# Score products of an attention kernel on 32x32 tiles of TensorE instead of 32x128 tiles

## The chip, the cores and the metric

The kernel runs on one core of one Trainium2 chip. The metric is the device time of one execution, in microseconds (us). Three executions of the kernel before took 753.29, 753.73 and 753.77 us; the median is 753.73 us.

## What is computed

x is 2048 rows of 640 (bf16). Two branches work on it, and a gate mixes them for each row:

```python
g = sigmoid((x * gate_w).sum(-1))
qkv = (x @ wqkv).reshape(S, 3, H, Dh)       # S=2048, H=32 heads, Dh=20
p = softmax(q @ k.T * Dh**-0.5)             # for each head
a = (p @ v).reshape(S, 640) @ wo
h = x @ w1 + b1                             # 640 -> 1536
b = (h * tanh(softplus(h))) @ w2            # 1536 -> 640
out = g * a + (1 - g) * b
```

## The kernel before, in words

**Layout.** x, k and q lie transposed in SBUF: `xT` with 640 rows in five blocks of 128, `kT` and `qT` with four heads stacked in the 128 partitions. Each head has a strip of 32 partitions, of which 20 hold data and the rest are zero. Four such heads are a quad; there are eight quads. Queries go in four chunks of 512 (QC), keys in 16 tiles of 128. A pair of quad and query chunk is a group (GROUPS, line 51), 32 groups in all, and a group has 32 units: one unit is one key tile for one pair of heads (`uinfo`, line 194), so there are 1024 units.

**A unit.** TensorE multiplies the strip of 32 rows of `kT` of a head (128 keys, the weights) with the strip of `qT` of that head (512 queries, the moving data) into one PSUM bank of 128 keys x 512 queries. A unit has two such products, for two heads, into the two banks of a slot. PSUM has eight banks: three slots of two, one bank that accumulates p @ v (ACCB), and one for other work (MISC). The scores of a slot are then turned into exp by ScalarE (line 946, 728 units) or by VectorE with an integer approximation of exp (line 966, 296 units), which makes three bf16 terms of a unit: the first by VectorE from PSUM, the two others from the first by GpSimd or VectorE (line 1065). Those results wait in the SBUF rings `EA` and `EC`.

**p @ v.** For each unit, `emit_pv` (line 662) multiplies 32 columns of `VA` (20 of v, a column of ones for the denominator, padding) with the exp tile of 128 keys x 512 queries, and accumulates in ACCB. The four heads of a quad go to the four strips of 32 partitions of that bank.

**Shapes on TensorE.** TensorE's array is addressed with a tile position (row, column). `mm` (line 299) is the only place that issues the matmuls; all of them carry line 300 in the profile. Three shapes occur:

- Score products use 32 rows x 128 columns at position (32r, 0), r being the head's place in the quad. Four of them, with four values of r, cover the array. The planner issues one unit (two products) or two units (four products) at a time.
- Everything else that multiplies, p @ v and the projections and the dense branch (through `mm4`, line 302), uses 128 rows x 32 columns at (0, 32q). Four of these cover the array.
- Transposes of x at the start (line 310) and in the last microseconds use the whole array, 128 x 128.

**The order of the work.** It is not found at run time. `make_plan` (line 220) simulates the five engines with a clock of its own (`Clock`, line 113) and writes down one list of calls, which is then issued in that order under a manual schedule; the waits follow from the data. `pe_run` (line 589) charges a burst of four products 217 ns, and 111 ns more when the kind of work changes between score products ("R"), products of 32 columns ("C") and transposes ("T"). `poll_pe` (line 826) asks in this order: score products if two slots are free or ScalarE is about to run dry, then p @ v if the exp rings are nearly full, then other work that is due, then p @ v. These charges are constants in the plan's code; the order of work that comes out doesn't depend on what `emit_score` (line 599) issues.

Of the kernel before, what the change touches and what calls it, by code (L numbers as in the profile page):

```python
# [10 lines left out]
P = 128  # L11
# [9 lines left out]
QC, NQC = 512, 4  # L21
# [172 lines left out]
def uinfo(n):  # L194
    g, k = divmod(n, 32)
    p, c = GROUPS[g]
    return g, p, c, k // 2, k % 2
# [22 lines left out]
def make_plan(K, par):  # L220
# [78 lines left out]
    def mm(o, l, r, first, last, pos):  # L299
        K.nc.tensor.matmul(o, lhsT=l, rhs=r, start=first, stop=last, tile_position=pos, skip_group_check=True)  # L300
# [298 lines left out]
    def emit_score(n, slot):  # L599
        g, p, c, kt, pair = uinfo(n)  # L600

        def fn():
            for t in range(2):
                r = 2 * pair + t
                mm(
                    K.ps[:, 2 * slot + t, :],
                    K.kT[32 * r : 32 * r + 32, p % 3, kt * P : (kt + 1) * P],
                    K.qT[32 * r : 32 * r + 32, p % 3, c * QC : (c + 1) * QC],
                    True,
                    True,  # L610
                    (32 * r, 0),
                )

        emit(fn)

# [733 lines left out]
```

## Time and profile before

| what | value | from |
|---|---|---|
| time of the profiled execution | 752.86 us | its result |
| its span, first to last instruction | 751.0 us | the page's head |
| around the span | 1.86 us | difference |
| median of three runs | 753.73 us | the times |
| mean granted clock of TensorE | 0.994 | the view of cores |
| busy: DVE, ACT, POOL | 587.7, 712.4, 532.0 us | part 1 |
| DMA | 41.86 MB, 56 GB/s on the mean | the page |
| instructions fetched by DMA (queue q8) | 82 packets, 1.34 MB | part 3 |

The page gives for each group of instructions its line, engine, shape and count, then the busy time with the mean duration of one in ns, then the time its engine stood idle before it. Matmuls overlap: one of 512 columns is shown as some 380 ns long, while the next can start after 216 ns or, on another tile, after a few ns. What tells the pace of TensorE is therefore the distance from start to start, not the duration, and these starts are in the trace's timeline.

### The profile page before, as it was taken

Reading aid. Unit: us, or ns where it says so; the run is one execution under the profiler, and the core shown is the slowest. Engines: PE = TensorE matmul, PEld = TensorE weight load, DVE = VectorE, ACT = ScalarE, POOL = GpSimd, SP = SyncE. Lnnn points to the kernel's source line nnn. Section 1 sums busy time; section 2 is a strip of 40 time slices with the busy share of each in tenths; the row PEclk is TensorE's granted clock in tenths of the full one; section 3 lists DMA queues with packets and bytes.
Section 4 is the critical chain, followed back from the end, with each engine's and each line's share of the span. In section 5 each row is a group of like instructions: output and inputs, shape, how many; then the busy total and the mean of one; then the engine's idle time right before and its main releaser. Section 6 shows DMA issues by size and latency. Waiting matters only on the chain.

```text
span 751.0 us, 25003 instructions
## 1 busy us (share of the span) xinstructions
PE 725.0 (97%) x10480; PEld 254.5 (34%) x10480; DVE 587.7 (78%) x758; ACT 712.4 (95%) x753; POOL 532.0 (71%) x496
## 2 busy tenths in 40 slices
PE   5989999999999999999999999999989999999997
PEld 3423333222233333333333333222323333333335
DVE  2486777878788787888878879888878887887794
ACT  2989999999999999999999999999999999999993
POOL 9155677766788676777767777777787688657773
PEclk8999999999999999999999999999999999999999
DMA  9242210002101001121111210000233110221132
GB/s 292 102 130 68 75 43 19 18 30 63 22 21 41 27 29 42 42 81 32 35 37 43 66 30 21 17 14 14 73 91 101 30 35 25 69 69 45 58 103 76
DMA packets 45722, 41.86 MB, mean 56 GB/s; under 512 B 20120, under 2 KB 39240, under 8 KB 45608
## 3 DMA queue, kind: packets, MB, share of 16 engines
q1 hardware_dynamic: 42984, 39.94, 17.9%
q8 instruction: 82, 1.34, 0.8%
q10 hardware_dynamic: 2624, 0.31, 0.3%
q14 instruction: 32, 0.26, 0.1%
HBM read 27.59 MB, written 12.38 MB: 53 GB/s over the span
## 4 chain that ended last, share of the span: by engine, by line
PE 77%; ACT 9%; DVE 8%; issue 3%; DMA 2%; POOL 0%; SPq 0%; ACTq 0%; DVEq 0%
PE ps L300 77%; ACT EA L946 8%; DVE EC L966 5%; DMA wv<-in_gate_w_dram 2%; DVE EC L1065 1%; DVE accs L989 1%; PE ps L310 0%; DVE VA L404 0%; DVE act L425 0%; POOL EC L1065 0%; DMA den<-accs 0%; DVE stg L357 0%; SPq L1146 0%; ACT L905 0%; DVE gt L936 0%
## 5 line engine op out<-in xcount | busy, mean ns | idle before, releaser
L946 ACT ACTIVATE EA<-ps 128x1024 bf16<-128x1024 f32 x728 | 680.0, 1045 | 24.0 <-PE ps L300 20.5
L1065 POOL TENSOR_SCALAR EC<-EC 128x1024 uint16<-128x1024 uint16 x426 | 468.7, 1101 | 202.7 <-DVE EC L966 176.8
L966 DVE TENSOR_SCALAR EC<-ps 128x1024 uint16<-128x1024 f32 x296 | 361.1, 1221 | 95.4 <-PE ps L300 72.6
L300 PE MATMUL ps<-qT,kT 32*128 32x512 bf16 x2048 | 290.4, 384 | 8.6 <-DVE EC L966 2.7
L300 PE MATMUL ps<-EC,VA 128*32 128x512 bf16 x1776 | 237.2, 384 | 1.7 <-DVE accs L989 1.1
L300 PE MATMUL ps<-EA,VA 128*32 128x512 bf16 x1456 | 207.4, 383 | 0.4 <-DVE accs L989 0.4
L300 PEld LDWEIGHTS <-kT 32*128 32x128 bf16 x2048 | 76.5, 91 | 262.5 <-issue 255.8
L300 PEld LDWEIGHTS <-VA 128*32 128x32 bf16 x3232 | 76.4, 95 | 92.3 <-issue 78.2
L1065 DVE TENSOR_SCALAR EC<-EC 128x1024 uint16<-128x1024 uint16 x166 | 93.4, 563 | 7.5 <-DVE EC L966 0.5
L300 PE MATMUL ps<-R,act 128*32 128x320 bf16 x1536 | 84.1, 302 | 0.1
L300 PE MATMUL ps<-xT,R 128*32 128x512 bf16 x960 | 79.3, 384 | 1.0 <-DVE act L425 1.0
L300 PEld LDWEIGHTS <-R 128*32 128x32 bf16 (+1 forms) x1728 | 41.7, 95 | 45.6 <-issue 34.9
L300 PEld LDWEIGHTS <-act 128*32 128x32 bf16 x1536 | 36.1, 95 | 36.4 <-issue 27.4
L300 PE MATMUL ps<-wv,xT 128*32 128x81 bf16 (+2 forms) x960 | 35.3, 263 | 5.9 <-DMA wv<-in_gate_w_dram 5.5
L425 DVE TENSOR_SCALAR act<-ps,b1f 128x512 bf16<-128x512 f32 x48 | 35.7, 744 | 3.1 <-PE ps L300 2.8
L357 DVE CAST stg<-ps 128x512 bf16<-128x512 f32 (+1 forms) x40 | 27.3, 683 | 8.8 <-PE ps L300 8.8
L300 PE MATMUL ps<-wk,R 128*32 128x320 bf16 (+1 forms) x640 | 33.6, 302 | 0.1
L300 PE MATMUL ps<-xT,wk 128*32 128x512 bf16 x360 | 32.8, 383 | 0.1
L1167 POOL TENSOR_TENSOR ons<-accs,rb 128x512 bf16<-128x512 f32 x24 | 31.1, 1294 | 2.5 <-DMA rb<-rd_d 1.1
L300 PE MATMUL ps<-xT,wq 128*32 128x512 bf16 x400 | 30.5, 382 | 1.1 <-DVE VA L404 1.1
L404 DVE CAST VA<-ps 128x80 bf16<-128x80 f32 (+2 forms) x48 | 16.3, 373 | 15.7 <-PE ps L300 15.7
L300 PEld LDWEIGHTS <-xT 128*32 128x32 bf16 x960 | 18.7, 99 | 20.0 <-issue 12.1
(69 smaller groups left out, 200.9 us busy)
## 6 DMA issues: line engine op xcount, KB each, us to landing
rb<-rd_d SPq DMA_DIRECT2D x124, 64.0 KB
qd<-stg SPq DMA_DIRECT2D x20, 128.0 KB
b_d<-bst SPq DMA_DIRECT2D x16, 160.0 KB
out_dram<-ost SPq DMA_DIRECT2D x16, 160.0 KB
kT<-kd SPq DMA_DIRECT2D x28, 80.0 KB
qT<-qd SPq DMA_DIRECT2D x28, 80.0 KB
stg<-b_d SPq DMA_DIRECT2D x13, 160.0 KB
kd<-stg SPq DMA_DIRECT2D x16, 128.0 KB
```

Of the source, the lines that this page charges most:

```text
L300: K.nc.tensor.matmul(o, lhsT=l, rhs=r, start=first, stop=last, tile_position=pos, skip_group_check=True)
L357: K.nc.vector.tensor_copy(out=K.stg[0:w, s, :], in_=bank(b)[0:w, :])
L404: K.nc.vector.tensor_copy(out=K.VA[:, t0 + i, h0 * VS : (h0 + nh) * VS].rearrange("p (h d) -> p h d", d=VS)[:, :, 0:DH], in_=src[:, i, 0 : ...
L425: K.nc.vector.tensor_scalar(out=K.act[:, f, (c % 2) * QC : (c % 2 + 1) * QC], in0=bank(b), scalar1=K.b1f[:, f : f + 1], scalar2=None, op0= ...
L946: lambda: K.nc.scalar.activation(K.EA[:, e, :], K.ps[:, 2 * slot : 2 * slot + 2, :].rearrange("p b n -> p (b n)"), ACT.Exp, scale=SCALE)
L966: lambda: K.nc.vector.tensor_scalar(out=K.EC[:, e, :], in0=K.ps[:, 2 * slot : 2 * slot + 2, :].rearrange("p b n -> p (b n)"), scalar1=CH_M ...
L989: emit(lambda: K.nc.vector.tensor_copy(out=K.accs[:, g % 2, :], in_=K.ps[:, ACCB, :]))
L1065: eng.tensor_scalar(out=K.EC[:, e, :], in0=K.EC[:, e0, :], scalar1=float(CH_ADD[k]), scalar2=1.0, op0=ALU.add, op1=ALU.mult)
L1167: gp_q.append((1350.0, lambda: K.nc.gpsimd.tensor_tensor(out=dst(), in0=K.accs[:, b, :], in1=K.rb[:, b, :], op=ALU.mult), lambda: pl.give( ...
```

## The change

Each score product of 128 keys becomes four products of 32 keys. Product q takes 32 columns of the same 32 rows of `kT`, streams the same 512 columns of `qT`, and writes partitions 32q to 32q+31 of the same PSUM bank, at tile position (32r, 32q). The loop over the strips q is inside the loop over the two heads t. So a unit issues 8 products with 8 weight loads instead of 2 with 2, and two units together 16 with 16 instead of 4 with 4. Nothing else is edited.

```diff
             for t in range(2):
                 r = 2 * pair + t
-                mm(
-                    K.ps[:, 2 * slot + t, :],
-                    K.kT[32 * r : 32 * r + 32, p % 3, kt * P : (kt + 1) * P],
-                    K.qT[32 * r : 32 * r + 32, p % 3, c * QC : (c + 1) * QC],
-                    True,
-                    True,
-                    (32 * r, 0),
-                )
+                for q in range(4):
+                    mm(
+                        K.ps[32 * q : 32 * q + 32, 2 * slot + t, :],
+                        K.kT[32 * r : 32 * r + 32, p % 3, kt * P + 32 * q : kt * P + 32 * q + 32],
+                        K.qT[32 * r : 32 * r + 32, p % 3, c * QC : (c + 1) * QC],
+                        True,
+                        True,
+                        (32 * r, 32 * q),
+                    )
```

The lists of instructions of both kernels stand in the same order on every engine. On TensorE 2048 score products with their loads become 8192, so that its list grows from 20955 to 33243 rows. The lists of the other engines don't change but for line numbers (every line behind the edit moves by one).

## The prediction

> **What bounds the kernel now.** I read the page's busy times, then the chain of work that ended last, then the groups of line 300, then TensorE's timeline.
>
> ```profile
> PE 725.0 (97%) x10480; PEld 254.5 (34%) x10480; DVE 587.7 (78%) x758; ACT 712.4 (95%) x753; POOL 532.0 (71%) x496
> PE 77%; ACT 9%; DVE 8%; issue 3%; DMA 2%; POOL 0%; SPq 0%; ACTq 0%; DVEq 0%
> L946 ACT ACTIVATE EA<-ps 128x1024 bf16<-128x1024 f32 x728 | 680.0, 1045 | 24.0 <-PE ps L300 20.5
> L300 PE MATMUL ps<-qT,kT 32*128 32x512 bf16 x2048 | 290.4, 384 | 8.6 <-DVE EC L966 2.7
> L300 PEld LDWEIGHTS <-kT 32*128 32x128 bf16 x2048 | 76.5, 91 | 262.5 <-issue 255.8
> L300 PEld LDWEIGHTS <-VA 128*32 128x32 bf16 x3232 | 76.4, 95 | 92.3 <-issue 78.2
> ```
>
> TensorE carries 77% of the chain, ScalarE (ACT) 9%, VectorE 8%. ACT is nearly as full (95%), so TensorE getting slower costs at once, while TensorE getting faster soon meets ACT. A busy share doesn't tell how tight TensorE is; start-to-start distances do. First a stretch of the dense branch mixed with attention (columns: start us, length us, group):
>
> ```profile
> 360.99 0.39 PE L300 MATMUL ps<-EC,VA 128*32 128x512 bf16 x4
> 361.20 0.31 PE L300 MATMUL ps<-R,act 128*32 128x320 bf16 x4
> 361.44 0.40 PE L300 MATMUL ps<-qT,kT 32*128 32x512 bf16 x4
> 361.77 0.59 PE L300 MATMUL ps<-R,act 128*32 128x320 bf16 x12
> 362.19 0.39 PE L300 MATMUL ps<-EA,VA 128*32 128x512 bf16 x4
> 362.40 0.39 PE L300 MATMUL ps<-EC,VA 128*32 128x512 bf16 x4
> 362.73 0.39 PE L300 MATMUL ps<-qT,kT 32*128 32x512 bf16 x2
> ```
>
> Bursts of 32-column products of 512 follow each other every 0.21 us (360.99, 361.20), which is the streaming of 512 columns, and those of 320 every 0.14. Into a score burst it takes 0.33 us (362.40 to 362.73), and out of it 0.33 (361.44 to 361.77). To the nanosecond, the medians in the trace are: 216 between bursts of 32 columns, 322 from such a burst of 512 to a score burst, 318 out of a score burst of two products and 325 out of one of four, 226 instead of 216 behind the first burst after a score burst. Products of one burst start 3.5 ns apart. So every number is a stream of 213 ns, plus 3.5 ns for each product behind the first, plus **a pause of 98 ns at each change of shape**; a change there and back costs 98 + 98 + 10 = 206 ns.
>
> Score bursts come in 717 visits: 416 of two products, 262 of four, 39 of several bursts. In all there are 496 bursts of two and 264 of four (992 + 1056 = 2048, the row's count). Of the 717 visits 662 start within 15 ns of that model, so 92% of them wait for nothing but TensorE itself.
>
> **Does the pause go?** The change keeps the columns of the shape (32 wide everywhere) and leaves the rows different (32 for scores, 128 for the rest). Before has no products of 32x32, so the pause is bounded by the nearest rows: 206 ns a visit if rows alone make it, nothing if columns alone do. The transposes (line 310) tell: they are 128x128, and differ from a score product in rows only.
>
> ```profile
> 19.49 0.39 PE L300 MATMUL ps<-qT,kT 32*128 32x512 bf16 x2
> 19.81 0.56 PE L310 MATMUL ps<-ident,act 128*128 128x128 bf16 x7
> 20.31 0.39 PE L300 MATMUL ps<-qT,kT 32*128 32x512 bf16 x2
> ```
>
> Both have all 128 columns; only rows change, and yet it takes 0.32 us out of the score burst (19.49 to 19.81), the same as to 32-column work. In the other direction two such changes take 151 and 152 ns from a transpose, which streams 53 ns: 98 again. From transposes to 32-column work, where columns alone change, it is 149. Each of the two by itself brings the whole pause. I take 98 ns unchanged on both sides: this edit saves nothing there. What speaks against it is that all these rows involve transposes, which may pause for a reason of their own.
>
> The Trainium skill, "TensorEngine Tiling (Array Packing)", section Key Properties, says that changing the tiling mode, and not just the tile, drains TensorE, and it lists 32x32 and 128x32 as different modes. By it the sum has no saving either; the transposes' 151 and 320 ns agree, and no run so far shows 32x32.
>
> **What the change adds.** A burst of two becomes eight products and a burst of four sixteen: 496 x 6 + 264 x 12 = 6144 more products with as many loads. The moving data of the sixteen tiles stream together, as four tiles of different rows do now, and four of different columns do. But the shape changes behind the last, so the last start counts: 318 to 325 ns for two more products shows 3.5 ns for each. 6144 x 3.5 = **21.5 us** on TensorE: 21 ns for a burst of two, 42 for one of four.
>
> The Trainium skill, "TensorE: Matmul & The Clock Gate", section The mechanism, gives some 4 ns between starts of tiles; by that the sum would be 24.6 us.
>
> What is hidden: where TensorE waits for ACT or VectorE anyway, the 21 or 42 ns vanish. 92% of visits have no such wait, which gives 19.8 us; by the chain's 77% it is 16.6. I take 18 between them. ACT and VectorE get their scores 21 to 42 ns later, which costs nothing of its own while TensorE is the bound.
>
> **Costs taken as nothing.** (1) Issuing. Sixteen pairs of load and product must be issued within a visit:
>
> ```profile
> 27.78 0.52 PE L300 MATMUL ps<-wv,xT 128*32 128x81 bf16 x36
> ```
>
> 36 products of 81 columns, with their loads, started within 0.32 us (0.52 less one duration of 0.20): 9 ns a pair, where streaming alone (36 ns for four) sets the pace. Sixteen pairs need 144 ns by that, less than the 213 of the stream. (2) Fetching instructions: 12288 more, 64 bytes each (1.34 MB over 20960), make 48 more packets of 16 KB. Each takes some 1.1 us in the trace, and one is needed every 5.8 us instead of 9.2; the shortest distance now is 3.6. It is covered by what TensorE has queued; uncovered it would be 48 x 1.1 = 53 us, which nothing in before hints at. (3) The loads: a load of 32 columns takes 95 ns and one of 128 takes 91, so smaller loads are not quicker. In the line above a strip gets a new load every 36 ns, so loads on a strip come at most 36 ns apart. If the loads for different rows of a strip really took turns at 36 ns, a visit's last product would start at 36 + 10.5 instead of 24.5 ns (eight), or 108 + 10.5 instead of 52.5 (sixteen): 496 x 22 + 264 x 66 ns = 28 us more. The score bursts of now, whose loads cover all strips for four different rows and start 3.5 ns apart, are the nearest row; I take nothing, and keep the 28 for the range.
>
> **Sum.** 752.86 + 18 = 770.9 us for the profiled execution; the median of the runs lies 0.87 higher, so 753.73 + 18 = **772 us**.
>
> **The rivals.**
> - *The pause goes* (faster). If columns alone cause it, TensorE loses 717 x 206 ns = 148 us of pauses and gains 21 of starts; it stops being the bound, deciding as soon as more than the 21 is saved. ACT then sets the pace: its exponentials start 949 ns apart on the mean (pauses over 3 us left out), 913 at the median and 903 at best, so 728 x 36 to 728 x 46 ns = 26 to 33 us at most could go, less what the fixed order, VectorE and start and end leave. I take 20: 734 us, between 722 and 748. For: the change from transposes to 32 columns pauses. Against: so do changes of rows. Chance 0.13.
> - *Loads take turns on a strip*: 21.5 + 28 = 50 us at most on TensorE, so 785 to 800 us. Chance 0.09.
> - *The sixteen tiles don't stream together.* If the row groups of a strip follow each other, a burst of two needs one more stream and one of four needs three: 496 + 792 = 1288 x 0.213 = 274 us, 1028 us in all; if the four strips of one row group take turns, each added product is a stream, 6144 x 0.213 = 1309 us, 2063 us in all. Against it: 32-column bursts use the same rows on four strips 3.5 ns apart, and score bursts use the same columns on four row groups 3.5 ns apart. Chance 0.03. The Trainium skill, "TensorE: Matmul & The Clock Gate", section The mechanism, states that a weight load overlaps running matmuls only when its row group differs, which would give the second of these times; the 3.5 ns inside 32-column bursts disagree.
> - *Nothing happens*: later starts are hidden, because the pause runs for each strip by itself. 753 to 755 us. Chance 0.05.
> - My forecast, pause stays and starts cost 3.5 ns: 0.70.
>
> **How the numbers follow.** About 0.2% (1.5 us) is what a measurement of this kernel can tell from no change. Slower by more than that: 0.70 + 0.09 + 0.03 = 0.82; within: 0.05; faster: 0.13. The forecast's own range is 762 to 778 (half of the 21.5 hidden; 4 ns a start and none hidden). The range reaches up to the loads taking turns, 800, and down to 755, which leaves out the pause going, the streams in turn and part of nothing happening: some 0.2.
>
> **What would show it.** In the profile after, the group of qT,kT should read 32*32 x8192, with starts of a burst of sixteen spread over some 52 ns. The distance into a score burst should stay at 322 ns, and out of it become 339 (eight) and 367 (sixteen). ACT's waits for line 300 should grow. I am wrong if the distance into score bursts falls to about 216, if starts lie further apart than 4 ns, or if ACT takes TensorE's place in the chain.

## The result and the profile after

The changed kernel takes 771.94 us (median of three, 770.99 to 773.62) against 753.73: a ratio of 1.0247, 95% interval 1.0218 to 1.0276. It is slower by 18.2 us, where 18 were forecast. A later measurement, five executions beside nine of the kernel before, gave 1.0249 (1.0232 to 1.0265). The profiled execution took 771.94 us with a span of 770.2.

The page after, in the order of the lines shown before: busy times, the chain by engine, ACT's exponentials, score products and their loads.

```profile
PE 744.4 (97%) x16624; PEld 269.9 (35%) x16624; DVE 587.9 (76%) x758; ACT 721.0 (94%) x753; POOL 532.9 (69%) x496
...
PE 73%; DVE 6%; ACT 4%; issue 2%; POOL 0%; DVEq 0%; ACTq 0%
...
L947 ACT ACTIVATE EA<-ps 128x1024 bf16<-128x1024 f32 x728 | 688.6, 1030 | 30.2 <-PE ps L300 24.0
...
L300 PE MATMUL ps<-qT,kT 32*32 32x512 bf16 x8192 | 310.3, 385 | 6.7 <-ACT EA L947 3.3
...
L300 PEld LDWEIGHTS <-kT 32*32 32x32 bf16 x8192 | 93.1, 87 | 261.9 <-issue 255.6
```

The 2048 products of 32*128 have become 8192 of 32*32, yet their busy time grew only from 290.4 to 310.3 us: the sixteen tiles do stream together. DVE, ACT and POOL do the same work as before, and ACT's waits for line 300 rose from 20.5 to 24.0 us. The two chains can't be compared by these shares: the chain of after reaches back only to 115 us from the start, that of before to the start, where ACT led for a while. From there to the end (111 us on in before) TensorE has 82% of the chain before and 86% after, ACT 6% and 5%. So TensorE was the bound and is a little more so.

The same place of the program on TensorE's timeline (start us, length us, group):

```profile
370.85 0.39 PE L300 MATMUL ps<-EC,VA 128*32 128x512 bf16 x4
371.07 0.31 PE L300 MATMUL ps<-R,act 128*32 128x320 bf16 x4
371.31 0.44 PE L300 MATMUL ps<-qT,kT 32*32 32x512 bf16 x16
371.67 0.59 PE L300 MATMUL ps<-R,act 128*32 128x320 bf16 x12
372.09 0.39 PE L300 MATMUL ps<-EA,VA 128*32 128x512 bf16 x4
372.31 0.39 PE L300 MATMUL ps<-EC,VA 128*32 128x512 bf16 x4
372.63 0.71 PE L300 MATMUL ps<-qT,kT 32*32 32x512 bf16 x16
```

Into the score burst it still takes 0.32 us (372.31 to 372.63), although both sides now have strips of 32 columns, and out of it 0.36 (371.31 to 371.67) where it was 0.33. To the nanosecond, medians of the two traces:

| distance from first start to first start | before | after |
|---|---|---|
| 32-column burst to score burst | 322 | 320 |
| score burst of one unit to 32-column burst | 318 (2 products) | 338 (8) |
| score burst of two units to 32-column burst | 325 (4) | 365 (16) |
| first to last start inside: one unit, two units | 3.5, 10 | 23.5, 50 |
| first 32-column burst behind scores to the next | 226 | 226 |

So TensorE needs 496 x 20 + 264 x 40 - 717 x 2 ns = 19.0 us more. To see how much of that arrives, I compared when the 728 exponentials of ACT start, which come in the same order in both kernels: from the 28th to the 700th the changed kernel falls behind by 16.5 us, from 2.6 us to 19.1 us. It does so evenly but for one step, 1.4 us between the 531st and the 536th. There the profile after has 3.4 us in which TensorE was granted half its clock, and the profile before has none at that place. Of the view of stretches, after and then before (start and end, length, busy time of PE, PEld, DVE, ACT and POOL, then the granted clock, the DMA share and GB/s):

```profile
567.60:571.00 3.40, 3.18 (x26) 1.00 (x25) 0.00 (x0) 2.91 (x4) 3.32 (x4) 0.50 0.52 146
```

```profile
548.00:556.00 8.00, 7.10 (x76) 2.48 (x75) 6.20 (x8) 7.93 (x8) 7.12 (x8) 1.00 0.41 118
```

Without that step 15.1 us are left. They stand against 17.8 us by the bursts of the stretch (458 x 20 + 249 x 40 - 666 x 2 ns): 85% reach the end in this execution. Whether the changed kernel meets the half clock more often than the one before isn't shown.

Most of the first 2.6 us is something else, namely a stop near 24 us. After, then before:

```profile
23.51 0.59 PE L300 MATMUL ps<-EA,VA 128*32 128x512 bf16 x5
26.00 0.40 PE L300 MATMUL ps<-EA,VA 128*32 128x512 bf16 x3 [1.90 <-issue]
```

```profile
23.50 0.60 PE L300 MATMUL ps<-EA,VA 128*32 128x512 bf16 x8
23.93 1.04 PE L300 MATMUL ps<-xT,wkp 128*32 128x512 bf16 x16
```

In the middle of eight p @ v products TensorE stands still for 1.90 us and waits for no engine ("issue"), at product 351 of its list (the first is 0; from start to start the stop is 2.06 us more than a stream). A packet of instructions landed 1.25 us before that product started.

### The profile page after: what moved, and what is told of

It is laid out like the page before. It is cut to its first block, busy times and chain, and to the rows that moved or that the text cites. A ratio compares the mean times of both kernels' runs of the same rounds, so it can differ in the third digit from the quotient of the medians.

```text
span 770.2 us, 37291 instructions
## 1 busy us (share of the span) xinstructions
PE 744.4 (97%) x16624; PEld 269.9 (35%) x16624; DVE 587.9 (76%) x758; ACT 721.0 (94%) x753; POOL 532.9 (69%) x496
## 3 DMA queue, kind: packets, MB, share of 16 engines
q1 hardware_dynamic: 42984, 39.94, 17.8%
## 4 chain that ended last, share of the span: by engine, by line
PE 73%; DVE 6%; ACT 4%; issue 2%; POOL 0%; DVEq 0%; ACTq 0%
PE ps L300 72%; DVE EC L967 4%; ACT EA L947 3%; ACT act L904 1%; DVE EC L1066 1%; DVE accs L990 1%; ACT L906 0%; POOL EC L1066 0%; DVE act L425 0%; DVE VA L404 0%; DVE stg L357 0%; ACT L904 0%; DVE ost L477 0%; PE ps L1110 0%; ACT dmy L906 0%
## 5 line engine op out<-in xcount | busy, mean ns | idle before, releaser
L947 ACT ACTIVATE EA<-ps 128x1024 bf16<-128x1024 f32 x728 | 688.6, 1030 | 30.2 <-PE ps L300 24.0
L300 PE MATMUL ps<-qT,kT 32*32 32x512 bf16 x8192 | 310.3, 385 | 6.7 <-ACT EA L947 3.3
L300 PEld LDWEIGHTS <-kT 32*32 32x32 bf16 x8192 | 93.1, 87 | 261.9 <-issue 255.6
L990 DVE COPY accs<-ps 128x512 f32<-128x512 f32 x32 | 21.9, 683 | 2.9 <-PE ps L300 2.9
```

Source lines behind the costliest of these rows:

```text
L947: lambda: K.nc.scalar.activation(K.EA[:, e, :], K.ps[:, 2 * slot : 2 * slot + 2, :].rearrange("p b n -> p (b n)"), ACT.Exp, scale=SCALE)
L990: emit(lambda: K.nc.vector.tensor_copy(out=K.accs[:, g % 2, :], in_=K.ps[:, ACCB, :]))
```

## The experiments

**Theory.** A change of tile shape makes TensorE pause for some 98 ns whichever side of the shape changes; the pause counts from the last start of the burst; starts are 3.3 ns apart; TensorE is the bound, so this reaches the end. **Rivals:** the pause hangs on columns, on overlapping areas or on the score products' own waits; the loss is the price of issuing or fetching more instructions, or a fixed price of the 32x32 shape.

**1. The pause by itself** (shapes): bursts of all shapes strung together, with nothing to wait for.

```diff
+    for X in (C, full(32, 128), full(32, 32), diag, full(64, 32), full(64, 64), full(128, 64), T, full(32, 64)):
+        for _ in range(8):
+            burst(*C)    # four products 128x32
+            burst(*C)
+            burst(*X)
```

> A kernel of TensorE bursts alone; it leaves out the whole computation and writes zeros. It strings together two bursts of 128x32 (or 128x128) products of 512 columns and one burst of another shape, eight times each. Theory (a change of tile shape pauses for 98 ns, whatever side changes, and the pause counts from the last start, 3.3 ns a product): two bursts of 128x32 216 ns apart; from them into any other shape 320 to 322 ns; out of 32x128 (4 tiles) 325, out of 32x32 365 with 16 tiles and 325 with 4 tiles, out of 64x32 and 32x64 (8 tiles) 338, out of 64x64 (4) 325, out of 128x64 (2) 318, out of 128x128 (1) 314. From plain 128x128 products, not transposes, into 32x128 or 64x128, where rows alone change, the same pause. Rival (columns alone pause; the transposes were a case of their own): 216 to 220 into 32x32 and 64x32 from 128x32, and into 32x128 from 128x128. Rival (overlap of the areas and not the shape): in the last part, where 64x32 tiles and 32x32 tiles lie on different rows and columns, they start a few ns apart; by the theory 310 to 330 ns apart, while two sets of 64x32 tiles on different rows and columns start a few ns apart.

Measured in ns, from first start to first start, medians of eight; "pause" is the distance out, less 213 of streaming, less the spread of starts:

| base | other shape, tiles | into | out of | spread | pause out |
|---|---|---|---|---|---|
| 128x32 | 128x32, 4 | 216 | 216 | 16 | none |
| 128x32 | 32x128, 4 | 322 | 325 | 10 | 102 |
| 128x32 | 32x32, 16 | 320 | 364 | 50 | 101 |
| 128x32 | 32x32, 4 on the diagonal | 320 | 324 | 10 | 101 |
| 128x32 | 64x32, 8 | 320 | 340 | 23.5 | 103 |
| 128x32 | 128x128, 1 | 321 | 319 | 0 | 106 |
| 128x32 | 64x64, 4 | 320 | 340 | 10 | 117 |
| 128x32 | 32x64, 8 | 318 | 352 | 23 | 116 |
| 128x32 | 128x64, 2 | 320 | 337 | 3 | 121 |
| 128x128 | 32x128, 4 | 312 | 327 | 10 | 104 |
| 128x128 | 64x128, 2 | 312 | 322 | 3 | 106 |

Every change of shape pauses, rows alone (64x32 and 32x32 against 128x32, 32x128 and 64x128 against plain 128x128) and columns alone (128x64 and 128x128 against 128x32). What counts is the tile and not how much of it is used: in the kernel before, products of 96 rows on tiles of 128x32 start 136 ns behind a burst of 128 rows and 320 columns of data, as another such burst does. The columns-only rival is out, and so is the doubt that the transposes were special. Overlap is out too: two tiles of 64x32 followed by four of 32x32 on other rows and other columns start 306 to 317 ns apart, two sets of 64x32 on other rows and columns 2 to 4 ns apart (from the last start of one set to the first of the other). The 306 to 317 are the first five pairs; behind them the granted clock is 0.5 and the distance goes to 533. The Trainium skill, "TensorEngine Tiling (Array Packing)", section Key Properties, has the rule that a change of mode, not of tile, drains TensorE, without a price; the table agrees with it.

What I had not expected is the third group: out of tiles 64 columns wide the pause is 14 to 20 ns longer. Their loads are longer too:

```profile
L41 PEld LDWEIGHTS <-w 32*32 32x32 bf16 x208 | 3.1, 88 | 11.2 <-issue 11.2
...
L41 PEld LDWEIGHTS <-w 32*128 32x128 bf16 x64 | 1.6, 90 | 6.8 <-issue 6.8
L41 PEld LDWEIGHTS <-w 32*64 32x64 bf16 x64 | 1.0, 101 | 3.4 <-issue 3.4
L41 PEld LDWEIGHTS <-w 64*64 64x64 bf16 x32 | 0.9, 103 | 3.4 <-issue 3.4
L41 PEld LDWEIGHTS <-w 128*64 128x64 bf16 x16 | 0.9, 106 | 3.4 <-issue 3.4
```

With 32 rows a load of 64 columns takes 101 ns, one of 32 takes 88 and one of 128 takes 90; with 64 rows it is 103 against 91 and 93, with 128 rows 106 against 98 and 96. In every row of the table with a pause, the pause out is 10 to 15 ns longer than the load of the other shape, so the two go together; no run changes the length of the load alone, so that the load is the cause is argued and not shown.

**2. Scores without a change of shape** (noswitch).

```diff
+            w = QC // (2 * k)            # k units are issued together
             for t in range(2):
-                r = 2 * pair + t
                 for q in range(4):
                     mm(
-                        K.ps[32 * q : 32 * q + 32, 2 * slot + t, :],
-                        K.kT[32 * r : 32 * r + 32, p % 3, kt * P + 32 * q : kt * P + 32 * q + 32],
-                        K.qT[32 * r : 32 * r + 32, p % 3, c * QC : (c + 1) * QC],
+                        K.ps[32 * q : 32 * q + 32, 2 * slot + t, 0:w],
+                        K.kT[:, p % 3, kt * P + 32 * q : kt * P + 32 * q + 32],
+                        K.qT[:, p % 3, c * QC : c * QC + w],
                         True,
                         True,
-                        (32 * r, 32 * q),
+                        (0, 32 * q),
```

> Scores by 128x32 products, the shape of all the other work, so that the shape changes no more. To keep the streaming the same, two products in a row on a strip take 256 queries each where one unit is issued, and four take 128 where two units are; it leaves out half or three quarters of the score columns (old values stay there), and adds up four heads. Theory (the pause belongs to the change of shape, and TensorE is the bound with ACT close behind): 216 to 230 ns into a score burst instead of 322, TensorE loses 717 x 206 ns = 148 us of pauses, ACT becomes the bound: 722 to 748 us, near 734, with ACT's share in the chain up. Rival (the pause belongs to the score products, to their waits or to kT and qT): distances stay near 320, 752 to 760 us.

733.53 us, ratio to before 0.9735 (0.9710 to 0.9760). A 32-column burst and the score burst behind it, the chain of this kernel, and TensorE's waits for ACT:

```profile
353.42 0.40 PE L300 MATMUL ps<-EC,VA 128*32 128x512 bf16 x4
353.64 0.41 PE L300 MATMUL ps<-qT,kT 128*32 128x256 bf16 x8
...
ACT 21%; PE 7%; issue 4%; DVE 3%; DMA 1%; SPq 1%; DVEq 0%; ACTq 0%
ACT EA L947 20%; PE ps L300 6%; DVE EC L967 2%; DMA den<-accs 1%; DMA wk<-in_A_wo_dram 1%; SPq L1147 0%; DVE EC L1066 0%; ACT act L904 0%; DVE act L425 0%; DVE accs L990 0%; DVE stg L357 0%; PE ps L1110 0%; DVE ost L477 0%; ACT L906 0%; SPq L245 0%
...
PE ps L300 <- ACT EA L947: 32.1, 130, 1.5
```

Where nothing is waited for, 32-column bursts are followed by score bursts after 214 to 216 ns (0.22 us from 353.42 to 353.64). With the same tensors, waits and slots the pause is gone, so it belongs to the change of shape. And now ACT heads the chain: it reaches back only to 471 us, and of the 259 us from there ACT has 59% and TensorE 18%, where before TensorE had 78% of the same part and ACT 8%. TensorE waits 32.1 us for ACT (2.5 before). So some 150 us of pauses are worth 20 us, as the rival of the prediction had it (734). That holds for the order of work as it is: the plan's constants still charge 111 ns for each change, and a plan made without that charge was not run.

**3. Half of the strips** (half32): a third of the added products, the shape kept.

```diff
-                for q in range(4):
+                for q in range(2):
```

> The changed kernel with only two of the four strips: half of the keys of each tile get no scores (the other PSUM partitions keep old values, set to zero once at the start). 4096 products of 32x32. Theory (3.3 ns for each start behind the first, in front of an unchanged pause): out of a score burst 324 ns (four products) and 338 (eight), against 318 and 325 before; into it 319 against 322; 496 x 6 + 264 x 13 - 717 x 2.4 ns = 4.7 us, so 755 to 759 us. Rival (a fixed price for each visit of the 32x32 shape, or of a shape that is tiled on both sides): as the change, 770 to 773.

(The edit also adds 24 products at the start, which set PSUM to zero; the kernel of experiment 2 has them too.) The median is 761.03 us, above the 755 to 759 expected. Of seven executions four lie at 761.03 to 761.11, with a mean granted clock of 0.991, and three at 756.57 to 758.85, with 0.995 to 0.997. The ratio is 1.0076 (1.0048 to 1.0105), that is 3.6 to 7.9 us. The distances are as expected: out of score bursts 324 to 325 (four products) and 338 (eight), into them 319 to 320, and 496 x 6 + 264 x 13 - 717 x 2 ns = 5.0 us. The fixed price, 770 us and more, is out.

**4. Strips of 64 columns** (cols64): a third of the added products.

```diff
-                for q in range(4):
+                for q in range(2):
...
-                        K.ps[32 * q : 32 * q + 32, 2 * slot + t, :],
+                        K.ps[64 * q : 64 * q + 64, 2 * slot + t, :],
...
-                        (32 * r, 32 * q),
+                        (32 * r, 64 * q),
```

> Score products on 32x64 tiles: two for each product of before, 2048 more instead of 6144. Theory (3.3 ns for each added start, in front of an unchanged pause): 6.8 us on TensorE, of which 84 to 92% reach the end: 759 to 760 us, 1.008 of before, a third of the change's loss; distance out of a score burst 324 (four products) and 338 (eight). Rival (a fixed price of column tiling for each visit, 18.2 us over 717 visits = 25 ns): 772. Rival (nothing before sixteen tiles): 754.

764.65 us, 1.0159 (1.0144 to 1.0175): a miss, twice the loss expected. The starts are as expected (10 ns inside four, 23 inside eight), but the distances out are 338 and 352 instead of 324 and 338, and 320 in. The missing 14 ns are as much as the loads are longer, as in experiment 1: score products here show 398 ns each where those of 32x32 show 385, loads 101 where those show 87. 496 x 20 + 264 x 27 - 717 x 2 ns = 15.6 us on TensorE, of which 12.1 arrive (78%). So starts are the whole price only between shapes whose loads are about equally long, as 32x128 (91 ns) and 32x32 (87) are.

**5. As many products, without the shape** (nsplit): 32x128 as before, four products of 128 queries for each one.

```diff
-            for t in range(2):
-                r = 2 * pair + t
-                for q in range(4):
+            for q in range(4):
+                for t in range(2):
+                    r = 2 * pair + t
                     mm(
-                        K.ps[32 * q : 32 * q + 32, 2 * slot + t, :],
-                        K.kT[32 * r : 32 * r + 32, p % 3, kt * P + 32 * q : kt * P + 32 * q + 32],
-                        K.qT[32 * r : 32 * r + 32, p % 3, c * QC : (c + 1) * QC],
+                        K.ps[:, 2 * slot + t, 128 * q : 128 * q + 128],
+                        K.kT[32 * r : 32 * r + 32, p % 3, kt * P : (kt + 1) * P],
+                        K.qT[32 * r : 32 * r + 32, p % 3, c * QC + 128 * q : c * QC + 128 * q + 128],
                         True,
                         True,
-                        (32 * r, 32 * q),
+                        (32 * r, 0),
```

> As many products and loads as the change (8192 for the scores), but of the shape before, 32x128, each over 128 queries instead of 512; four rounds after each other on each tile. Theory (the number of products costs only by the starts that lie behind the last stream): a burst streams four times 56 instead of 216 ns, some 7 ns more, 760 x 7 = 5 us, and up to 2 us of waiting for instructions near the start, as seen at 24 us in the profile after: 756 to 761 us. Rival (issuing or fetching 60% more instructions is what costs): as the change, 770 to 774.

764.76 us, 1.0157 (1.0142 to 1.0173): between the two expected times, and neither. From the start of a score burst to the next 32-column burst it takes 326 ns with one unit (318 before), as expected, but 352 with two units (325 before). The starts tell why. Of sixteen products in a burst, eight of a unit in front of eight of the next one in the list, the trace has these starts in ns (medians; unit one on two rows of tiles, unit two on the two others):

```
unit one:   0   3 |  66  70 | 122 126 | 178 181
unit two:  27  30 |  93  97 | 149 152 | 205 208
```

Which product is which shows in their semaphores: a wait for a slot stands at 0 and again at 27 ns, and the signals that a unit is done at 181 and at 208. The second unit starts 27 ns behind the first, about eight pairs of load and product at 3.3 ns; the stream of the tiles that started last then ends 27 ns later. 496 x 8 + 264 x 27 = 11.1 us, and 12.2 were measured. So 8192 products cost as such neither what the change costs (18.2 us) nor nothing: what counts is how late the last tile starts streaming. This kernel also stops at product 351, for 0.60 us in the view that gave 1.90 (0.77 from start to start, where the other had 2.06).

**6. The changed kernel again** (after_again) and **with the old shape for the first 64 units** (late).

> The changed kernel once more, beside the others. Theory: 771 to 774 us; the stop of 2.06 us on TensorE near 24 us, with no wait for another engine and with a packet of instructions under way, comes again. Rival (an accident of the one profile): it is not there.

771.49 us. The stop is not in this profile. The packet of instructions landed at about the same time, but TensorE came to product 351 some 3 us later, since it was granted half its clock from 17.0 to 27.2 us (its distances out of score bursts are 555 to 556 ns in that stretch). The 28th exponential is 3.7 us late all the same.

```diff
-                for q in range(4):
+                w = P if n < 64 else 32
+                for q in range(P // w):
...
```

> The changed kernel, but the first 64 of the 1024 units on 32x128 as before. Theory (stops of TensorE at product 351, of 2.06 us in the profile after and 0.77 in the one with queries split, come from instructions that arrive late, since the list has grown by then): no stop there, and the starts of 64 units less (some 1.2 us), so 768.5 to 770.5 us, and the exponentials from the 28th on shifted by 1 us or less against before, not by 3 or 3.8. Rival (the start differs from run to run by the first transfers alone): 770.5 us, with a shift of 0 to 4 us that has nothing to do with the shape.

769.35 us, 1.0215 (1.0187 to 1.0243). There is no stop, and the 28th exponential comes 0.2 us behind before; from it to the 700th the kernel loses 15.9 us. That is what the theory says of the start, but the interval overlaps that of the changed kernel. That late instructions cause the stop in the changed kernel is made likely, not shown: two kernels with long lists stop at the same product, 1.25 and 1.27 us after a packet of instructions landed, and one with a shorter list doesn't stop. Where TensorE came to that product only 1.67 us after the landing (after_again), there was no stop either. What the start costs on the mean, between 0 and 4 us, stays open.

**7. Fewer visits** (nohurry): the pauses of before are worth 20 us; can the plan save some?

```diff
-    "thr": 270.70346323743667,
+    "thr": 1e9,
...
-    "thr_2": 301.0904425828448,
+    "thr_2": 1e9,
```

> The kernel before with two numbers of its plan changed (thr and thr_2, line 59 and 80, to 1e9), so that the planner issues a single unit's scores only when TensorE has nothing else, and otherwise waits for two free slots. The whole computation is done. By the list of instructions score products then come in 601 visits instead of 717, and 59 bursts of filling products are added, 10713 products in all instead of 10477. Theory (each visit costs 206 ns of pauses, and TensorE is the bound): 116 x 206 ns = 24 us less of pauses on TensorE, less 59 x 216 ns = 13 us of filling where TensorE is idle anyway: 735 to 752 us if ACT gets its scores in time. Rival (the early single units are what keeps ACT fed, and ACT takes the place of TensorE as the bound before the 24 us are reached): 754 us or more, with ACT's waits for line 300 well over 24 us.

838.73 us, 1.1119 (1.1084 to 1.1154). Time and waits are as the rival has them, and by far:

```profile
ACT EA L946 <- PE ps L300: 117.7, 201, 8.7
...
PE ps L300 <- ACT EA L946: 27.1, 86, 1.7
```

ACT waits 117.7 us for scores (20.5 before), and TensorE's mean granted clock falls to 0.955 (0.994). In the chain TensorE still leads, with 62% against 17% for ACT, so ACT has not taken its place as the bound; each now waits for the other. By that clock TensorE ran some 75 of the 837 us at half speed (0.045 x 837 x 2, an estimate), and the new plan also moves exponentials from ACT to VectorE (726 and 811 instructions, 753 and 758 before). How the 86 us divide among these isn't shown. What is shown is that this plan, with 116 visits fewer, leaves ACT without scores far longer. No version here that does the whole work beats the kernel before.

## Why the prediction was right, point by point

- **The pause stays** (0.70): right. The step was argued from transposes; experiment 1 shows the same for plain products, 99 ns into and 104 to 106 out of shapes that differ in rows only, and experiment 2 that it goes when the shape doesn't change.
- **A visit costs 206 ns of pauses**: a little too small. The pause into a score burst is 98 ns, but out of it 318 less 213 less 3.5 is 101.5, so not every distance comes out of the model. By the distances, less the 216 of a stream without a change, a visit costs 106 + 102 + 10 = 218 ns with two products and 225 with four, some 158 us in all instead of 148. This enters only the rival in which the pause goes, not the forecast.
- **Each start costs 3.5 ns, 21.5 us in all**: right in kind, a little too much. Starts are 3.3 ns apart (50 ns over fifteen steps), and each of 717 entries is 2 ns shorter: 19.0 us. A third of the added products (experiment 3) cost 5.7 us by the ratio, with 5.0 by its distances. The Trainium skill, "TensorE: Matmul & The Clock Gate", section The mechanism, has some 4 ns; the trace's 3.3 decides.
- **18 of 21.5 us reach the end** (84%): the share is right, 85% in the long middle part (15.1 of 17.8 us). It was a choice between 77% and 92%, so its closeness is luck.
- **Fetching taken as nothing**: not quite. 1.9 us of the profiled execution are a stop without any wait near the start, most likely for instructions.
- **That 18.2 us came out where 18 were forecast** is in part luck. The profiled execution after is 19.2 us longer in its span than that before: 2.6 up to the 28th exponential, the stop among them, 16.5 in the middle part, 1.4 of them at half clock, and 0.1 behind it. The later starts account for some 16 of these, less than the 18 forecast, because they were 19.0 and not 21.5; the stop and the half clock, which are not in the sum, made up for it. How the 18.2 between the medians divide, no trace shows.
- **Sixteen tiles stream together, loads take no turns**: right. Fifteen steps take 50 ns; with loads on a strip taking turns at 36 ns they would have taken 118.
- **Out of bursts 339 and 367, into them 322**: 338, 365 and 320.
- **ACT is close behind**: right, 733.5 us without the pause (experiment 2) against 734. The 26 to 33 us at most were worked out, the 20 taken from them was a guess, so the half microsecond between them is luck.
- **Smaller loads are not quicker**: the 95 and 91 ns compared there belong to tiles of different rows. With 32 rows a load of 32 columns takes 87 ns and one of 128 takes 91, so it is a little quicker; nothing in the sum hangs on it.

## What to carry to other kernels

What pauses TensorE in all these runs is a change of tile shape, rows or columns; keeping one of the two the same saves nothing, and only the same shape on both sides does. The pause runs from the start of the last tile, so where shapes alternate, use the fewest products that fill the array, and beware of tiles 64 columns wide, which cost 14 to 20 ns more at each exit. Read a busy engine by start-to-start distances, and price what it would win against the engine behind it: here some 150 us of pauses were worth 20. And before reading a difference of two profiles as one effect, look where it arises: a stop of 1.9 us and a stretch at half clock of 1.4 stood in it beside the effect.

## What the runs showed of the hardware that was not expected

- Products on different rows of tiles don't start in the order of the list: in experiment 5 the ninth product starts 27 ns behind the first, before the third (66 ns), which waits for its own tile. The Trainium skill, "TensorE: Matmul & The Clock Gate", section The mechanism, states that matmuls start strictly in program order; this trace disagrees.
- A load of 64 columns takes longer (101 to 106 ns) than one of 32 (88 to 98) and than one of 128 (90 to 96), and out of tiles of 64 columns the pause is 14 to 20 ns longer.
- With 6144 more products and their loads in the list, TensorE stood still for 1.90 us and, in experiment 5, for 0.60 us at the same product near the start; in a second profile of the changed kernel it did not.
